# Expert-output row scatters declared independent of each other in a chunk-select attention and top-1 routing kernel

## The chip, the cores and the metric

The kernel runs on one core of one Trainium2 chip. The metric is device time in microseconds (us), the median of several runs. The engines are named as in the profile: PE is the matrix engine, PEld its weight load, DVE the vector engine, ACT the scalar engine, POOL the GpSimd engine and SP the sync engine; POOL and SP issue the transfers that matter here, and 16 DMA engines carry them.

## What is computed

An attention over 4 x 8 heads of 768 positions keeps six chunks of 32 keys per query; its output, reshaped to 3072 tokens of 512 numbers, goes through a mixture of eight experts of which each token uses one.

```python
def _moe_ref(x, w_gate, w1, w2):          # x: 3072 x 512
    logits = x @ w_gate
    expert_idx = np.argmax(logits, axis=1)
    ...
    for e in range(E):                    # 8 experts
        mask = expert_idx == e
        h = np.maximum(x[mask] @ w1[e], 0.0)      # 512 -> 1024
        ye = h @ w2[e]                            # 1024 -> 512
        out[mask] = gate_w[mask, None] * ye
```

## The kernel before

The first part (to about 262 us of the span) is the attention. As token rows are finished they are scattered by expert into a scratch table in HBM, `xs_dram`, with 258 four-byte words a row: the token's 512 bf16 numbers, its gate weight and its number. Some steps of the second part are begun before the first ends.

The second part works through 31 tiles of up to 128 tokens, `j` = 0 to 30, each of one expert. For each tile there are five steps:

- `gather(j)`: an indirect transfer, issued by POOL, brings 128 rows of `xs_dram` into one of eight buffers (four named `xg`, two halves of `KTE`, two of `QSB`). Rows beyond the expert's count have an index out of bounds and are skipped.
- `x_in(j)`: a transposing transfer, issued by SP, turns the tile into `xT` (128 x 512 bf16, kept in the other `KTE` and `QSB`), and DVE copies the token numbers to `ti` (L541 to L547); where a row is no token's the number is made out of bounds.
- `up(j)`: 8 matmuls of 512 columns into `ph` (L558), ACT's Relu into `h` (L562), and a transposing transfer on SP from `h` to `hT` (128 x 1024 bf16, L564).
- `down(j)`: 8 matmuls into `py` (L571), for which there is one buffer; ACT scales `py` into `y` (L575; four buffers in turn).
- still in `down(j)`: an indirect transfer, issued by POOL, scatters the 128 rows of `y` (2 KB each) to `out` in HBM (L576). Rows out of bounds are skipped. Padding makes the last tiles hold few tokens or none.

The order on PE and on SP is the program's; on the other engines the scheduler sets it. The steady order is `gather(j+4)`, `up(j)`, `x_in(j+3)`, `down(j-2)`:

```python
for j in range(NA + 2, JT + 2):
    order += [(up, j), (x_in, j + 3), (down, j - 2)]
for f, j in order:
    if j >= JT:
        continue
    if f is up and j + 4 < JT:
        gather(j + 4)
    f(j)
```

Every engine works through its own list in order, so an instruction that waits holds up all behind it on that engine. The waits are set by a dependency tracker. Two writes to one tensor are ordered by it: it does not know which rows an indirect transfer writes, so each scatter into `out` waits until the scatter before it has landed. A transfer also takes one of eight semaphores in turn (DMASW0 to DMASW7 for POOL's), and waits for the transfer that used it eight transfers earlier.

Of the kernel before, what the change touches and what calls it, by code (L numbers as in the profile page):

```python
# [21 lines left out]
def kernel(  # L22
# [10 lines left out]
    nc = tc.nc  # L33
# [533 lines left out]
    def down(j):  # L567
        hT, wo = fs[j]["hT"], fs[j]["wo"]
        py = ps_o.tile([128, DM], FP32, tag="o")
        for c in range(NFC):  # L570
            nc.tensor.matmul(py[:], lhsT=hT[:, c, :], rhs=w_all[:, ds(wo + (W1W + c * DM), DM)],  # L571
                             start=(c == 0), stop=(c == NFC - 1))
        nm = ("k", "q", "v", "v")[j % 4]
        y = ld.tile([128, DM], FP32, tag=nm, bufs=2 if nm == "v" else 1, name="y")
        nc.scalar.activation(y[:], py[:], AF.Copy, bias=0.0, scale=fs[j]["gt"])  # L575
        nc.gpsimd.indirect_dma_start(  # L576
            out=out[:], out_offset=bass.IndirectOffsetOnAxis(ap=fs[j]["ti"], axis=0),
            in_=y[:], in_offset=None, bounds_check=NTOK - 1, oob_is_err=False,
        )

# [14 lines left out]
    with tc.manual_schedule(engines={PE}):  # L597
# [60 lines left out]
        with tc.manual_schedule(engines={SP}):  # L658
# [10 lines left out]
            up(2)  # L669
            x_in(5)  # L670
            down(0)
            r[1]()
            gather(6)
# [4 lines left out]
            for j in range(3, NA):  # L678
                order += [(up, j)] + [(x_in, j + 3)] * (j + 3 < NA) + [(down, j - 2)]
            order += [(down, NA - 2), (x_in, NA), (x_in, NA + 1), (x_in, NA + 2), (up, NA),  # L680
                      (x_in, NA + 3), (down, NA - 1), (up, NA + 1), (x_in, NA + 4)]
            for j in range(NA + 2, JT + 2):
# [44 lines left out]
```

## Time and profile before

| | us |
|---|---|
| median of 3 runs | 414.83 (412.9 to 415.79) |
| profiled execution | 411.02 |
| its span, first to last instruction | 409.3 |
| PE busy in the span | 351.9 |
| ACT busy | 242.0 |
| DVE busy | 230.0 |
| POOL busy | 187.6 |

The mean granted clock of PE is 0.959 of full speed. The busy shares are means over two parts with different limits; DVE is nearly idle in the second one. What the second part waits for is read from the order of its instructions in time and from the row at the end of the idle stretches, which names what came last.

### The profile page before, as it was taken

What the parts mean: (1) busy time and instruction counts of PE and PEld (TensorE: products, weight loads), DVE (VectorE), ACT (ScalarE), POOL (GpSimd) and SP (SyncE); (2) the same over time, 40 slices, a digit from 0 to 9 for tenths busy, and PEclk for the clock granted to TensorE, in tenths of its full rate; (3) what the DMA queues carried; (4) which work ended last, traced back from release to release, by engine and by line L of the source; (5) the groups of instructions that cost most, each with busy time, mean ns of one, the idle gap of its engine ahead of it and who ended that gap; (6) DMA issues with size and microseconds to landing.
All of it is one profiled execution on the core that took longest, in us unless ns stands there. A gap on an engine that the chain in (4) does not pass through costs nothing.

```text
span 409.3 us, 7510 instructions
## 1 busy us (share of the span) xinstructions
PE 351.9 (86%) x2272; PEld 175.0 (43%) x2272; DVE 230.0 (56%) x783; ACT 242.0 (59%) x403; POOL 187.6 (46%) x304
## 2 busy tenths in 40 slices
PE   2688999999989999799999798899799879988710
PEld 1244455545545545445545444444244334333300
DVE  8449789889978989968989985670000000000000
ACT  2487779779769777849777845244244434443300
POOL 9124244333674424753433746646454353534131
PEclk9889999999999999989999989999899999999975
DMA  9265999898799899699799452479879878877610
GB/s 178 56 117 113 172 184 146 151 204 163 156 197 165 182 169 176 144 197 180 142 172 189 91 105 53 117 136 195 182 183 163 180 133 202 162 174 147 141 43 0
DMA packets 143366, 60.99 MB, mean 149 GB/s; under 512 B 127963, under 2 KB 136157, under 8 KB 143328
## 3 DMA queue, kind: packets, MB, share of 16 engines
q1 hardware_dynamic: 125408, 31.09, 40.6%
q0 software_dynamic: 17920, 29.42, 37.0%
q8 instruction: 20, 0.33, 0.3%
q14 instruction: 18, 0.15, 0.2%
HBM read 56.54 MB, written 11.30 MB: 166 GB/s over the span
## 4 chain that ended last, share of the span: by engine, by line
PE 45%; DMA 21%; ACT 12%; issue 9%; DVE 8%; POOL 2%; POOLq 1%; SPq 0%; ACTq 0%; DVEq 0%
DMA out_dram<-y,ti 16%; PE po L310 11%; PE ps L288 6%; PE ph L558 5%; PE pu L233 5%; PE py L571 3%; ACT Pr L293 3%; PE pu L338 3%; PE pt L370 3%; ACT QSB L262 3%; ACT QSB L261 3%; PE pu L343 2%; PE pt L209 2%; PE pt L241 2%; DMA xg<-xs_dram,grow 2%
## 5 line engine op out<-in xcount | busy, mean ns | idle before, releaser
L322 DVE TENSOR_TENSOR Pa<-Pa,Pr 128x768 f32<-128x768 f32 (+2 forms) x112 | 82.2, 734 | 4.4 <-PE po L310 2.4
L293 ACT ACTIVATE Pr<-ps 128x768 f32<-128x768 f32 (+2 forms) x112 | 65.3, 628 | 3.4 <-PE ps L288 3.1
L297 POOL TENSOR_SCALAR_AFFINE_SELECT Pr<-Pr 128x256 f32<-128x256 f32 x80 | 33.6, 438 | 72.8 <-ACT Pr L293 71.9
L571 PE MATMUL py<-w_all,hT 128*128 x248 | 58.6, 379 | 4.2 <-ACT y L575 2.6
L576 POOL DMA_INDIRECT out_dram<-y,ti x31 | 30.8, 994 | 63.1 <-DMA out_dram<-y,ti 23.2
L288 PE MATMUL ps<-QSB,KTE 128*128 128x384 bf16 (+2 forms) x288 | 49.2, 295 | 3.5 <-ACT QSB L262 2.5
L288 PEld LDWEIGHTS <-KTE 128*128 128x128 bf16 x288 | 24.3, 98 | 35.8 <-issue 27.7
L571 PEld LDWEIGHTS <-hT 128*128 128x128 bf16 x248 | 24.2, 98 | 35.0 <-issue 3.2
L558 PE MATMUL ph<-w_all,KTE 128*128 x128 | 31.9, 394 | 6.2 <-DMA KTE<-xg 3.7
L435 POOL DMA_INDIRECT xs_dram<-xrow,sli x24 | 26.7, 1111 | 13.8 <-DVE sli L428 5.2
L558 PE MATMUL ph<-w_all,QSB 128*128 x120 | 28.1, 379 | 3.8 <-PE py L571 2.9
L546 DVE TENSOR_TENSOR ti<-xg,inv_i 128x1 int32<-128x1 int32 x12 | 1.9, 160 | 51.4 <-DMA xg<-xs_dram,grow 51.4
L346 ACT ACTIVATE ud<-pu 128x384 f32<-128x384 f32 x16 | 7.8, 491 | 34.2 <-PE pu L343 34.2
L293 ACT ACTIVATE Pa<-ps 128x768 f32<-128x768 f32 x32 | 25.9, 811 | 3.2 <-PE ps L288 2.6
L172 POOL DMA_DIRECT2D w_all<-in_moe_w_dram x32 | 24.5, 764 | 0.0
L558 PEld LDWEIGHTS <-KTE 128*128 128x128 bf16 x128 | 12.7, 100 | 23.8 <-issue 7.1
L201 DVE TENSOR_REDUCE kmx<-pt 128x12 f32<-128x384 f32 x32 | 17.7, 554 | 7.5 <-PE pt L199 7.4
L218 POOL CAST QSB<-qT 64x384 bf16<-64x384 f32 x32 | 16.0, 508 | 11.6 <-DVE qT L216 11.2
L244 DVE TENSOR_TENSOR ubm<-pt,cbias 128x144 f32<-128x144 f32 x32 | 8.6, 302 | 21.6 <-PE pt L241 21.5
L529 POOL DMA_INDIRECT xg<-xs_dram,grow x16 | 16.9, 1056 | 6.9 <-issue 6.6
L558 PEld LDWEIGHTS <-QSB 128*128 128x128 bf16 x120 | 11.6, 97 | 19.4 <-issue 5.0
L372 DVE TENSOR_TENSOR xrow<-pt,rec 128x384 bf16<-128x384 f32 x32 | 17.6, 552 | 1.9 <-DMA xs_dram<-xrow,sli 1.1
(296 smaller groups left out, 668.2 us busy)
## 6 DMA issues: line engine op xcount, KB each, us to landing
w_all<-in_moe_w_dram POOLq DMA_DIRECT2D x32, 512.0 KB, 7.3
out_dram<-y,ti POOLq DMA_INDIRECT x31, 3.3
t__187<-in_k_dram SPq DMA_DIRECT2D x2, 192.0 KB, 3.1
t__190<-in_q_dram SPq DMA_DIRECT2D x2, 192.0 KB
t__193<-in_v_dram SPq DMA_DIRECT2D x2, 192.0 KB, 4.1
t__202<-in_v_dram SPq DMA_DIRECT2D x2, 192.0 KB, 4.6
t__196<-in_k_dram SPq DMA_DIRECT2D x2, 192.0 KB, 3.2
t__199<-in_q_dram SPq DMA_DIRECT2D x2, 192.0 KB, 3.4
```

What stands on the lines that cost most here:

```text
L172: d = nc.gpsimd.dma_start(out=dst, in_=src.rearrange("(c p) f -> p c f", p=128))
L201: nc.vector.tensor_reduce(s["kmx"][:, ts(hf, 12)], pk, AX.X, ALU.max)
L233: nc.tensor.matmul(pu[64 * hf:64 * hf + 64, :], lhsT=w_[:], rhs=s[f"{nm}{hf}"][:], start=(nm == "qT"), stop=(nm == "qA"), skip_group_check ...
L288: nc.tensor.matmul(pv[:, hd, :], lhsT=kte[:, hd, ts(kb, 128)], rhs=qsb[:, hd, ds(qb * 384 + 384 - w, w)], start=True, stop=True, skip_grou ...
L293: nc.scalar.activation(P[:, :, ds(c0, w)], pv, AF.Exp)
L297: nc.gpsimd.affine_select(out=pd, in_=pd, pattern=[[0, 2], [1, 128]], compare_op=ALU.is_ge, fill=0.0, base=0, channel_multiplier=-1)
L310: nc.tensor.matmul(po[64 * hd:64 * hd + 64, 384 - w:384], lhsT=vt[:, kb, hd, :], rhs=P[:, hd, ds(c0, w)], start=first, stop=last and n == ...
L322: nc.vector.tensor_tensor(acc[:, :, 384 - w:384], acc[:, :, 384 - w:384], P[:, :, ds(c0, w)], ALU.add)
L435: d = nc.gpsimd.indirect_dma_start(out=xs_dram[:], out_offset=bass.IndirectOffsetOnAxis(ap=sli[:, u:u + 1], axis=0), in_=bst[b][f"xrow{u % ...
L558: nc.tensor.matmul(ph[:, fh, :], lhsT=xT[:, c, :], rhs=w_all[:, ds(wo + (c * F + fh * 512), 512)], start=(c == 0), stop=(c == NDC - 1), sk ...
L571: nc.tensor.matmul(py[:], lhsT=hT[:, c, :], rhs=w_all[:, ds(wo + (W1W + c * DM), DM)], start=(c == 0), stop=(c == NFC - 1))
L576: nc.gpsimd.indirect_dma_start(out=out[:], out_offset=bass.IndirectOffsetOnAxis(ap=fs[j]["ti"], axis=0), in_=y[:], in_offset=None, bounds_ ...
```

## The change

The scatters of `y` are put into a group `y` whose members are declared free of dependencies on one another, because no token is in two tiles. Nothing else is edited.

```diff
         y = ld.tile([128, DM], FP32, tag=nm, bufs=2 if nm == "v" else 1, name="y")
         nc.scalar.activation(y[:], py[:], AF.Copy, bias=0.0, scale=fs[j]["gt"])
-        nc.gpsimd.indirect_dma_start(
+        d = nc.gpsimd.indirect_dma_start(
             out=out[:], out_offset=bass.IndirectOffsetOnAxis(ap=fs[j]["ti"], axis=0),
             in_=y[:], in_offset=None, bounds_check=NTOK - 1, oob_is_err=False,
         )
+        tc.declare_no_dep(d.ins, group="y", reason="every token is in one tile")
+        tc.add_to_no_dep_group("y", d.ins)
```

PE, DVE, ACT and SP keep their instructions in the same order. POOL's list changes in its waits, and in one place in its order. The first place is the middle of the second part, where gathers (L529) and scatters (L576) alternate. Before:

```order
L529 DMA KTE1_169<-xs_dram_63,grow_183 128x258 [waits DMAHW2_49,DMASW3_49]
L529 DMA QSB1_173<-xs_dram_63,grow_183 128x258 [waits DMAHW4_49,Activation_49]
L576 DMA out_0_dram<-y_3968,ti_3808 3072x512 [waits DMASW5_49,DMASW2_49]
L576 DMA out_0_dram<-y_4013,ti_3844 3072x512 [waits DMASW5_49,Activation_49]
L529 DMA QSB1_173<-xs_dram_63,grow_183 128x258 [waits DMAHW6_49,DMASW7_49]
L576 DMA out_0_dram<-y_4071,ti_3974 3072x512 [waits DMASW6_49,DVE_49,Activation_49]
L529 DMA xg0_3507<-xs_dram_63,grow_183 128x258 [waits DMAHW2_49,DMASW1_49]
L576 DMA out_0_dram<-y_4107,ti_3977 3072x512 [waits DMASW0_49,DVE_49,Activation_49]
```

and in the changed kernel, the same stretch of POOL's list:

```order
L529 DMA KTE1_169<-xs_dram_63,grow_183 128x258 [waits DMAHW2_49,DMASW3_49]
L576 DMA out_0_dram<-y_3968,ti_3808 3072x512 [waits DMASW4_49,Activation_49]
L529 DMA QSB1_173<-xs_dram_63,grow_183 128x258 [waits DMAHW4_49,DMASW5_49]
L576 DMA out_0_dram<-y_4013,ti_3844 3072x512 [waits DMASW6_49,Activation_49]
L529 DMA QSB1_173<-xs_dram_63,grow_183 128x258 [waits DMAHW6_49,DMASW7_49]
L576 DMA out_0_dram<-y_4071,ti_3974 3072x512 [waits DMASW0_49,DVE_49,Activation_49]
L529 DMA xg0_3507<-xs_dram_63,grow_183 128x258 [waits DMAHW2_49,DMASW1_49]
L576 DMA out_0_dram<-y_4107,ti_3977 3072x512 [waits DMASW2_49,DVE_49,Activation_49]
```

The scatter of y_3968 (tile 6) moved ahead of the gather of tile 14. The DMA semaphore that each scatter waits for was the one of the scatter before it; it is now the one that it takes itself, last used eight transfers earlier, which is four scatters earlier.

The second place is the end of POOL's list, the last six scatters (tiles 25 to 30). Before:

```order
L576 DMA out_0_dram<-y_4680,ti_4492 3072x512 [waits DMASW7_49,DVE_49,Activation_49]
L576 DMA out_0_dram<-y_4710,ti_4528 3072x512 [waits DMASW0_49,DMASW1_49,DVE_49,Activation_49]
L576 DMA out_0_dram<-y_4740,ti_4564 3072x512 [waits DMASW1_49,DVE_49,Activation_49]
L576 DMA out_0_dram<-y_4770,ti_4600 3072x512 [waits DMASW2_49,DMASW3_49,DVE_49,Activation_49]
L576 DMA out_0_dram<-y_4784,ti_4636 3072x512 [waits DMASW3_49,DVE_49,Activation_49]
L576 DMA out_0_dram<-y_4798,ti_4669 3072x512 [waits DMASW4_49,DMASW5_49,DVE_49,Activation_49]
```

and in the changed kernel:

```order
L576 DMA out_0_dram<-y_4680,ti_4492 3072x512 [waits DMASW0_49,DVE_49,Activation_49]
L576 DMA out_0_dram<-y_4710,ti_4528 3072x512 [waits DMASW1_49,DVE_49,Activation_49]
L576 DMA out_0_dram<-y_4740,ti_4564 3072x512 [waits DMASW2_49,DVE_49,Activation_49]
L576 DMA out_0_dram<-y_4770,ti_4600 3072x512 [waits DMASW3_49,DVE_49,Activation_49]
L576 DMA out_0_dram<-y_4784,ti_4636 3072x512 [waits DMASW4_49,DVE_49,Activation_49]
L576 DMA out_0_dram<-y_4798,ti_4669 3072x512 [waits DMASW5_49,DVE_49,Activation_49]
```

Nothing moved here; each scatter lost the wait for the one before it and keeps those for its own `y` (ACT), its own `ti` (DVE) and the transfer eight earlier.

## Rows read from the trace of the kernel before

**Rows 1.** The page's part 4, chain that ended last: shares by line.

```profile
DMA out_dram<-y,ti 16%; PE po L310 11%; PE ps L288 6%; PE ph L558 5%; PE pu L233 5%; PE py L571 3%; ACT Pr L293 3%; PE pu L338 3%; PE pt L370 3%; ACT QSB L262 3%; ACT QSB L261 3%; PE pu L343 2%; PE pt L209 2%; PE pt L241 2%; DMA xg<-xs_dram,grow 2%
```

**Rows 2.** POOL's timeline, 279 to 409 us: start, duration, instruction, idle before.

```profile
292.41 1.01 POOL L576 DMA_INDIRECT out_dram<-y,ti  x1 [3.10 <-issue]
...
308.95 0.99 POOL L576 DMA_INDIRECT out_dram<-y,ti  x1 [3.75 <-ACT y L575]
310.24 1.05 POOL L529 DMA_INDIRECT QSB<-xs_dram,grow  x1 [0.30 <-issue]
313.84 1.01 POOL L576 DMA_INDIRECT out_dram<-y,ti  x1 [2.54 <-DMA out_dram<-y,ti]
...
398.88 0.97 POOL L576 DMA_INDIRECT out_dram<-y,ti  x1 [1.88 <-DMA out_dram<-y,ti]
401.82 0.97 POOL L576 DMA_INDIRECT out_dram<-y,ti  x1 [1.97 <-DMA out_dram<-y,ti]
```

**Rows 3.** ACT's timeline in the second part.

```profile
299.50 0.69 ACT L575 ACTIVATE y<-py,QSB 128x512 f32<-128x512 f32 x1 [0.75 <-PE py L571]
...
383.79 1.02 ACT L562 ACTIVATE h__4757<-ph 128x1024 bf16<-128x1024 f32 x1 [2.17 <-PE ph L558]
385.52 0.69 ACT L575 ACTIVATE y<-py,KTE 128x512 f32<-128x512 f32 x1 [0.70 <-PE py L571]
...
391.95 0.69 ACT L575 ACTIVATE y<-py,QSB 128x512 f32<-128x512 f32 x1 [2.91 <-DMA out_dram<-y,ti]
```

**Rows 4.** PE's timeline, 289 to 392 us.

```profile
294.14 3.55 PE L558 MATMUL ph<-w_all,KTE 128*128 x8 [2.12 <-DMA KTE<-xg]
...
304.43 1.89 PE L558 MATMUL ph<-w_all,QSB 128*128 x8
...
314.87 1.89 PE L558 MATMUL ph<-w_all,KTE 128*128 x8
...
319.71 1.89 PE L558 MATMUL ph<-w_all,QSB 128*128 x8 [0.45 <-PE py L571]
...
381.82 1.89 PE L558 MATMUL ph<-w_all,KTE 128*128 x8 [0.97 <-PE py L571]
383.54 1.89 PE L571 MATMUL py<-w_all,hT 128*128 x8
...
389.09 1.89 PE L571 MATMUL py<-w_all,hT 128*128 x8 [0.94 <-ACT y L575]
```

**Rows 5.** SP's timeline: the transposing transfer of one `x_in`.

```profile
316.34 1.19 SPq L541 DMA_TRANSPOSE QSB<-QSB  x1
```

**Rows 6.** Windows: us, busy time of each engine, granted clock, DMA share, GB/s.

```profile
300.00:304.00 4.00, 4.00 (x20) 1.75 (x18) 0.16 (x1) 2.23 (x3) 3.06 (x3) 1.00 0.83 200
304.00:308.00 4.00, 4.00 (x20) 1.79 (x19) 0.16 (x1) 1.71 (x2) 1.02 (x1) 1.00 1.07 230
308.00:312.00 4.00, 4.00 (x20) 1.83 (x19) 0.16 (x1) 2.09 (x3) 2.05 (x2) 1.00 0.94 196
300.00:320.00 20.00, 18.94 (x88) 8.37 (x86) 0.79 (x5) 9.73 (x12) 9.37 (x10) 1.00 0.98 185
320.00:340.00 20.00, 17.18 (x78) 7.41 (x77) 0.80 (x5) 7.90 (x10) 9.13 (x10) 1.00 0.80 166
340.00:360.00 20.00, 17.96 (x81) 7.78 (x80) 0.64 (x4) 8.55 (x10) 10.12 (x10) 1.00 0.90 184
360.00:380.00 20.00, 18.02 (x81) 7.67 (x79) 0.80 (x5) 8.55 (x10) 9.18 (x9) 1.00 0.72 154
```

**Rows 7.** Issue to landing: scatters of `y`; transposes into `hT`; gathers (284 to 390 us).

```profile
DMA to landing us min/median/max: 2.1/3.3/4.7
...
DMA to landing us min/median/max: 3.1/3.5/4.5
...
DMA to landing us min/median/max: 2.6/3.5/6.1
```

**Rows 8.** The page's part 3: POOL's queue, with packets, MB, share of 16 engines.

```profile
q0 software_dynamic: 17920, 29.42, 37.0%
```

## The prediction

> **What bounds the kernel now.** Start with the chain of work that ended last. Its largest single share, 16%, is the landing of scatters into `out`, before any engine's line [rows 1]. Busy times alone would not have told this: in the second part PE is busy for 17 to 19 of every 20 us [rows 6]. Next, POOL's timeline shows how the scatters come to be there. The scatter at 308.95 us is that of tile 7, whose `y` ACT wrote from 299.50 us on [rows 2, 3]: it starts 8.8 us after its data were ready, because the scatter before it had first to land. (The row names ACT as what came last; ACT had long been done, so it was another.) The next one starts at 313.84, named as waiting for the landing of its predecessor [rows 2]. So scatters form a chain of their own, of issue (1.0 us) and landing (3.3 us in the middle case [rows 7]), and POOL's list makes others share it: the gather of tile 15 stands right behind the scatter of tile 7 and starts at 310.24 [rows 2]; its `x_in` can start only at 316.34 [rows 5]; its `up` starts at 319.71, 4.84 us after the one before [rows 4].
>
> That is to be set against PE's own pace. A block of eight matmuls takes 1.72 us when the next follows directly (381.82 to 383.54), so an `up` and a `down` take 3.44 us [rows 4]. From `up(11)` at 304.43 to `up(14)` at 314.87 three steps took 10.44 us, 3.48 each; from `up(11)` to `up(30)` at 381.82 nineteen took 77.39 us, 4.07 each [rows 4]. PE thus loses 0.63 us a step, all of it after `up(14)`.
>
> At the end there is nothing but the chain. `down(30)` starts at 389.09 and needs 1.89 us, to 390.98 [rows 4], yet the last scatter starts at 401.82, its predecessor at 398.88 [rows 2].
>
> **The change, part by part.** No instruction is added or removed. What goes is one wait per scatter; what remains is each one's own `y`, its own `ti`, and the transfer eight earlier, which in the steady order is the scatter of four tiles earlier. Four steps are at least 13.8 us, and the longest landing shown is 4.7 us [rows 7], so I cost that wait at nothing; if landings rose above 12 us it would be felt.
>
> *The end.* `y` followed its matmuls by 0.09 us where it waited for nothing else: `down(28)` starts at 383.54, so it ends at 385.43, and `y` starts at 385.52 and takes 0.69 [rows 3, 4]. For tile 30: 390.98 + 0.09 + 0.69 = 391.76, after which its scatter may start, against 401.82: **10.05 us** saved. Before, `y` of tile 30 itself waited, to 391.95, for a scatter to free its buffer [rows 3]; that goes too. The `down`s of the end are 2.7 us or more apart and a scatter keeps POOL 0.97 us, so POOL is no queue there. What comes after the last scatter moves with it unchanged. This term rests on PE's end staying where it is; the next term moves it.
>
> *The nineteen steps.* Gathers no longer stand behind a waiting scatter. They come some 8 us earlier relative to `up`, `x_in` and with it the next `hT` (behind it in SP's list) come on time, and PE's own pace is next: 19 x 3.44 = 65.4 us, 12.0 saved. That is one end. The other is the DMA engines. A step with all its rows moves 132 KB of gather, 131 KB of `x_in`, 262 KB of `hT` and 262 KB of scatter, 787 KB. The busiest twelve microseconds, 300 to 312, with DMA shares of 0.83, 1.07 and 0.94, moved 200, 230 and 196 GB/s, 209 in the mean [rows 6]: 3.77 us for such a step, 71.6 for nineteen, 5.8 saved. Not all steps are full: the four windows from 300 to 380 us moved 185, 166, 184 and 154 GB/s [rows 6], 13.8 MB in 80 us or 19.7 steps of 4.07, that is 700 KB, and 3.35 us at 209 GB/s. So on average the DMA engines can just keep PE's pace, and while full tiles pass they can't quite. Between 3.44 and 3.77 I take **3.6 us** a step: 3.48 was really run for three steps under this load, but with gathers fetched ahead, so that pace was partly paid from a lead. 19 x 3.6 = 68.4, **9.0 us** saved.
>
> The Trainium skill ("DMA: Bandwidth & Descriptors", sections "Bandwidth" and "Latency and other measured facts") gives about 358 GB/s for HBM transfers of a core and 261 GB/s for a transposing transfer; an estimate from these is 393 KB / 261 + 394 KB / 358 = 2.6 us for a full step, well under 3.44, and by it the whole 12.0 us would come back, a time near 393. The best 4 us window here, 230 GB/s over all queues [rows 6], does not bear that out; I stay with the windows.
>
> *The steps ahead of it.* The scatter at 292.41 (tile 3) idled 3.10 us first [rows 2]; it will be issued up to that much earlier, when the `x_in` is under way for which PE waits 2.12 us before `up(8)` at 294.14 [rows 4]. Its 262 KB at 230 GB/s are 1.1 us, the most that it can delay that transfer; the least is nothing. A gain there I exclude, since that `x_in` waits for no scatter into `out`. I take 0.3 us, nearer to nothing, since the scatter's bytes would mostly have passed by then. The exchange of tile 6's scatter with tile 14's gather costs one issue of 1.0 us on POOL, hidden, because the gather is needed two steps later.
>
> **Sum:** 9.0 + 10.05 - 0.3 = 18.75 us. Against the profiled execution's own 411.02 that is 392.3; that execution was 3.8 us below the median of the runs, so for the median I take the difference: 414.83 - 18.75 = **396.1 us**. With the bounds: at best 12.0 + 10.05, 392.8; at worst 5.8 + 10.05 - 1.1 = 14.75, 400.1.
>
> **The rivals.** *The DMA engines become the bound.* Without the chain, scatter, gather and two transposing transfers of a step meet more often, and all of them stretch. For it: shares of 0.9 and more already, and at 1.07 the rate rose only to 230 GB/s [rows 6]. Against: the average step needs 3.35 us. At 3.77 to 4.0 us a step it gives 5.8 to 1.4 us in place of 9.0, so 399.3 to 403.7. The Trainium skill (the same page, "Issuing engines are not separate DMA queues") says that transfers from any engine run on the same 16 DMA engines, which is this rival's premise; the share above 1 beside a nearly level rate agrees.
>
> *Slower: the gathers land late behind free scatters.* Both go through POOL's one queue [rows 8], so a gather issued 1.3 us after a scatter lies behind its bytes. There is a loop: scatter of `j-3`, gather `j+4`, `x_in(j+4)`, `hT` of `j+2` behind it on SP, `down(j+2)`, `y`, scatter of `j+2`: five steps. Its length is 0.99 + 0.30, a gather's landing 3.5 (6.1 at most), 1.19 on SP, `hT` 3.5 (4.5 at most), 1.89, 0.09 and 0.69 [rows 2 to 5, 7]: 12.2 us, at most 15.8, against 17.2 for five steps of PE. To make the kernel slower by 1% it would have to eat the end's 10.05 us and 4.15 more, 0.75 us a step, so 4.82 a step and 24.1 a loop: gathers would have to land 15 us after issue. Time then 419 or more. Nothing in the rows comes near.
>
> *The change does nothing, or its gain is handed on.* The waits for eight transfers earlier could act as the old one did, or steps grow so that PE ends later by what the end saves: 411 to 419. For the first, a landing of over 12 us would be needed; for the second, 4.6 us a step.
>
> **How the numbers follow.** A measurement of this kernel can tell about 1%, 4.1 us, from no change. Forecast (3.44 to 3.68 us a step): 62%. DMA bound (3.68 to 4.0): 32%. Nothing or handed on: 4%. Slower: 2%. So faster 0.94, same 0.04, slower 0.02. The range goes from 391.5 (PE's pace, with 1.3 us for the spread of the runs) to 402, which takes in most of the DMA rival and leaves its last part and the two others outside.
>
> **What would show it.** In the changed kernel's profile, scatters should start within 0.1 us of their `y` or directly behind a gather, and no row should name the landing of `out` as what POOL waits for. The distance from `up(11)` to `up(30)` over 19 should be about 3.6; 3.44 proves PE the bound, 3.77 and more the DMA engines, with `hT` landing in over 4.5 us and DMA shares near 1. The last scatter should start 0.8 us after the last matmul. I am wrong in the first term if another wait holds the last scatters, in the second if transposes land so late that PE idles before `down`, or if `x_in` waits for gathers still.

## The result, and the profile after

The changed kernel took 391.93 us (median of 4 runs, 391.16 to 393.09), the kernel before, run beside it, 415.31 (4 runs, 412.9 to 418.19): a ratio of 0.944, 95% interval 0.937 to 0.950. The forecast was 396.1. The profiled execution took 393.09, its span is 391.4, against 411.02 and 409.3 before. In three later sets of runs the kernel before came to 412.0 to 412.8, and the changed kernel, in two of them, to 398.11 (ratio 0.967, 0.962 to 0.971) and 398.53 (0.968, 0.963 to 0.973). A ratio is that of the means of fast runs, those not over 1.5% above the fastest of their kernel, while a median is of all runs. So the gain is real, and its size moved between occasions; both facts are taken up below.

The page of the changed kernel: the shares by engine and line of the chain that ended last (part 4), and the scatters' row in part 5 (busy time and mean ns, then idle time before them and who ended it). It answers to [rows 1].

```profile
POOL out_dram L576 4%; POOL xg L529 2%; DMA KTE<-xs_dram,grow 2%; POOL QSB L529 1%; POOL KTE L529 1%; DMA QSB<-xs_dram,grow 1%; DMA xg<-xs_dram,grow 1%; DMA out_dram<-y,ti 1%; POOL xs_dram L435 0%; POOLq L724 0%; POOLq L576 0%; DVE ti L546 0%; POOLq L529 0%; DVEq L546 0%
...
L576 POOL DMA_INDIRECT out_dram<-y,ti x31 | 31.2, 1006 | 44.6 <-ACT y L575 42.8
```

The landing of scatters fell from 16% of that chain to 1%. Scatters now wait 42.8 us in all for their own `y`, which is harmless: it is the time until there is something to scatter. No scatter of `y` names the landing of `out` any more.

POOL's timeline of the changed kernel, as [rows 2]:

```profile
289.89 1.02 POOL L576 DMA_INDIRECT out_dram<-y,ti  x1 [0.31 <-issue]
...
308.65 1.02 POOL L576 DMA_INDIRECT out_dram<-y,ti  x1 [2.82 <-ACT y L575]
309.97 1.04 POOL L529 DMA_INDIRECT xg<-xs_dram,grow  x1 [0.30 <-issue]
...
381.18 0.97 POOL L576 DMA_INDIRECT out_dram<-y,ti  x1 [1.74 <-ACT y L575]
383.89 0.97 POOL L576 DMA_INDIRECT out_dram<-y,ti  x1 [1.74 <-ACT y L575]
```

The first row is the scatter of tile 3, 2.5 us earlier than before (292.41). The scatter of tile 8 starts at 308.65; it was 313.84 before. The gather behind it follows after 0.30 us, and the last scatter starts at 383.89 in place of 401.82.

PE's timeline, as [rows 4], with `up(8)`, `up(11)`, `up(14)`, `up(30)` and `down(30)`:

```profile
296.46 3.57 PE L558 MATMUL ph<-w_all,KTE 128*128 x8 [5.07 <-DMA KTE<-xg]
...
307.43 1.89 PE L558 MATMUL ph<-w_all,QSB 128*128 x8
...
318.55 1.89 PE L558 MATMUL ph<-w_all,KTE 128*128 x8 [0.60 <-PE py L571]
...
373.80 1.89 PE L558 MATMUL ph<-w_all,KTE 128*128 x8
...
380.95 1.89 PE L571 MATMUL py<-w_all,hT 128*128 x8 [0.82 <-ACT y L575]
```

From `up(11)` to `up(30)` it is 66.37 us, 3.49 a step against 4.07 before: 11.0 us saved. `down(30)` ends at 382.84, and the last scatter starts 1.05 us later, 10.84 before: 9.8 saved. But `up(11)` itself came 3.0 us later than before (307.43 against 304.43): `up(8)` waited 5.07 us for its `xT`, against 2.12. The sum, 11.0 + 9.8 - 3.0 = 17.8, is the difference of the spans (17.9).

The windows of the changed kernel, as [rows 6], show what bounds it now:

```profile
300.00:320.00 20.00, 19.40 (x88) 8.53 (x86) 0.64 (x4) 9.58 (x11) 9.49 (x10) 0.97 0.87 183
320.00:340.00 20.00, 20.00 (x95) 9.08 (x93) 1.02 (x6) 10.06 (x12) 11.31 (x11) 1.00 0.91 208
340.00:360.00 20.00, 20.00 (x95) 9.02 (x94) 0.96 (x6) 9.78 (x12) 12.22 (x12) 1.00 0.88 192
```

PE is busy for 20.00 of 20 us at a granted clock of 1.00; it was 17.18 and 17.96. From 320 to 340 us the DMA engines move 208 GB/s, as much as in the busiest twelve microseconds before (209), while PE loses nothing.

### The profile page after: what moved, and what is told of

Read it like the earlier page. It is cut to its first block, busy times and chain, and to the rows that moved or that the text cites. A ratio compares the mean times of both kernels' runs of the same rounds, so it can differ in the third digit from the quotient of the medians.

```text
span 391.4 us, 7508 instructions
## 1 busy us (share of the span) xinstructions
PE 349.7 (89%) x2272; PEld 175.3 (45%) x2272; DVE 229.7 (59%) x783; ACT 242.1 (62%) x403; POOL 187.9 (48%) x304
## 5 line engine op out<-in xcount | busy, mean ns | idle before, releaser
L576 POOL DMA_INDIRECT out_dram<-y,ti x31 | 31.2, 1006 | 44.6 <-ACT y L575 42.8
L529 POOL DMA_INDIRECT xg<-xs_dram,grow x16 | 16.8, 1053 | 7.0 <-issue 6.0
L370 PE MATMUL pt<-ident_f,ot 128*128 128x128 f32 x96 | 17.1, 288 | 1.4 <-ACT KTE L204 0.3
```

Of the source, the lines that this page charges most:

```text
L529: d = nc.gpsimd.indirect_dma_start(out=xg_bufs[j % XB].bitcast(I32), out_offset=None, in_=xs_dram[:], in_offset=bass.IndirectOffsetOnAxis( ...
L576: d = nc.gpsimd.indirect_dma_start(out=out[:], out_offset=bass.IndirectOffsetOnAxis(ap=fs[j]["ti"], axis=0), in_=y[:], in_offset=None, bou ...
```

## The experiments

Unless a number says otherwise, all are compared with the kernel before, run beside them. In the first set those had a median of 411.96 us (11 runs), in the second 412.83 (7), in the third 412.31 (17). Spans are those of the profiled execution.

**Which scatters matter.** Three kernels declare only some of the scatters independent; all scatters stay members of the group.

```diff
-        tc.declare_no_dep(d.ins, group="y", reason="every token is in one tile")
+        if j >= 6:
+            tc.declare_no_dep(d.ins, group="y", reason="every token is in one tile")
```

with `j >= 6` (the first six stay in the chain), `j >= 25` (only the last six are free) and `j < 25` (only the last six are chained).

> Only the scatters of tiles 6 to 30 are free; those of tiles 1 to 5 still wait each for the one before. Theory (the freed early scatters crowd the transposing transfers of tiles 8 to 10, so that PE stood for 5.07 us before up(8) in the changed kernel against 2.12 before): up(8) starts near 294 again and the kernel takes about 389 us, 3 less than the changed kernel. Rival (a chance stall of the DMA engines fell there, whoever issues what): up(8) is as late as in the changed kernel, or varies, and the time is 392.

> Only the scatters of tiles 25 to 30 are free. Theory (two separate gains, 10 us at the end and the rest in the steps): the steps keep their 4.07 us, the last scatter starts about 1 us after PE's last matmul, 405 us. Rival (the gain at the end needs free scatters all along): 410 us or more.

> The scatters of tiles 0 to 24 are free, those of tiles 25 to 30 wait each for the one before. Theory (the 10 us at the end were a lag of two tiles gathered over all steps; a chain of six that starts without lag keeps up with tiles that come 3.45 or 2.7 us apart): 393 to 395 us. Rival (the end is serial landings by themselves): six landings in a row again cost about 10 us, 402.

Measured: free from 6 on 397.48 us (6 runs; ratio 0.962, 0.956 to 0.968), the last six free 401.60 (4 runs; 0.977, 0.969 to 0.984), the last six chained 403.95 (4 runs; 0.981, 0.974 to 0.987).

The expected times had counted from 391.93. All profiles of this set have a pause of PE near 280 us, some 7 us long, which those of the first two kernels don't have and which is taken up below. So the times alone decide little here: 397.48 fits neither expectation, and 403.95 is near the rival's 402. What is compared is the distances from `up(11)` on.

With the last six free, POOL's timeline, the scatters of tiles 24 to 30:

```profile
380.07 0.97 POOL L576 DMA_INDIRECT out_dram<-y,ti  x1 [3.12 <-DMA out_dram<-y,ti]
381.34 0.97 POOL L576 DMA_INDIRECT out_dram<-y,ti  x1 [0.30 <-issue]
...
385.17 0.97 POOL L576 DMA_INDIRECT out_dram<-y,ti  x1 [0.30 <-issue]
387.54 0.97 POOL L576 DMA_INDIRECT out_dram<-y,ti  x1 [1.39 <-ACT y L575]
390.25 0.97 POOL L576 DMA_INDIRECT out_dram<-y,ti  x1 [1.74 <-ACT y L575]
```

The first of these rows, tile 24, is the last that waits for a landing. It starts 11.7 us after PE had finished that tile's `down` (366.50 + 1.89 = 368.39). The next four are free and leave behind one another, 1.28 us apart; from tile 29 on each waits for its own `y` alone, and the last starts 1.05 us after PE's end (387.31 + 1.89 = 389.20). So what stands at the end is a queue of finished tiles, and freeing a few scatters works it off in 5.1 us. The theory's 4.07 us a step was wrong: it was 3.63 (`up(11)` at 311.20, `up(30)` at 380.16), for a reason that the kernel before shows below. With the same pause this profile's span, 397.7, is that of the whole change, 398.1; by the medians the last six free are 3.5 us slower (401.60 against 398.11).

With the last six chained, the end of POOL's timeline:

```profile
376.92 0.97 POOL L576 DMA_INDIRECT out_dram<-y,ti  x1 [3.83 <-DMA out_dram<-y,ti]
382.35 0.97 POOL L576 DMA_INDIRECT out_dram<-y,ti  x1 [4.46 <-ACT y L575]
385.80 0.97 POOL L576 DMA_INDIRECT out_dram<-y,ti  x1 [2.48 <-DMA out_dram<-y,ti]
388.66 0.97 POOL L576 DMA_INDIRECT out_dram<-y,ti  x1 [1.89 <-DMA out_dram<-y,ti]
391.60 0.97 POOL L576 DMA_INDIRECT out_dram<-y,ti  x1 [1.97 <-DMA out_dram<-y,ti]
```

PE ends at 384.65 + 1.89 = 386.54 there, so the last scatter starts 5.06 us later: 4.0 more than free, not the rival's 10 more. The same kernel in the second set:

> Scatters of tiles 0 to 24 free, the last six chained, on the same chip as the changed kernel. Theory (corrected by the first run of this kernel, whose last scatter began 5.1 us after PE's last matmul against 1.05): 3 to 5 us over the changed kernel. Rival (six landings in a row cost what they cost before): 10 us over it.

It took 402.08 us (4 runs; 0.978, 0.972 to 0.983). Its last matmuls and its last scatter:

```profile
389.35 1.89 PE L571 MATMUL py<-w_all,hT 128*128 x8 [0.82 <-ACT y L575]
392.98 0.97 POOL L576 DMA_INDIRECT out_dram<-y,ti  x1 [1.97 <-DMA out_dram<-y,ti]
```

The scatter came only 1.74 us after PE's end (391.24). Six landings in a row therefore cost between 0.7 and 4.0 us at the end. The other 6 to 9 us of the kernel before were brought along from the steps. The median lies 4.0 us above that of the whole change in the same set, more than 0.7; its `up(11)` also came 1.6 us later in the profile, so the 4.0 aren't all the chain's.

**Two chains in place of one.** Scatters of even and of odd tiles each keep their own chain:

```diff
-        tc.declare_no_dep(d.ins, group="y", reason="every token is in one tile")
-        tc.add_to_no_dep_group("y", d.ins)
+        tc.declare_no_dep(d.ins, group=f"y{(j + 1) % 2}", reason="every token is in one tile")
+        tc.add_to_no_dep_group(f"y{j % 2}", d.ins)
```

> Each scatter waits for the one two tiles earlier. Theory (a chain binds only where issue and landing, 4 to 4.5 us, exceed the step; two chains have 6.9 us for that): same as the changed kernel, 392 us. Rival (any wait of a scatter for a landing holds up the gathers behind it): a third or more of the gain is lost, 400 us or more.

Measured: 401.17 us (4 runs; 0.974, 0.968 to 0.981). `up(11)`, `up(30)`, `down(30)` and the last scatter:

```profile
315.62 1.89 PE L558 MATMUL ph<-w_all,QSB 128*128 x8
381.23 1.89 PE L558 MATMUL ph<-w_all,KTE 128*128 x8
388.38 1.89 PE L571 MATMUL py<-w_all,hT 128*128 x8 [0.83 <-ACT y L575]
391.32 0.97 POOL L576 DMA_INDIRECT out_dram<-y,ti  x1 [1.74 <-ACT y L575]
```

The steps ran at (381.23 - 315.62) / 19 = 3.45 us, and the last scatter started 1.05 us after PE's end (388.38 + 1.89). From `up(11)` on this is the whole change. The time is the rival's, 400 or more, but not for the rival's reason: no scatter of `y` names a landing. What was lost against 391.93 lies ahead of `up(11)`, which came at 315.62. Part of it is the pause. Against the whole change with the pause (398.11) 3.1 us are left; in the profiles the very first scatter, ahead of any chain, already started 2.3 us later (274.15 against 271.81). So the chain hurts because one issue and one landing, 1.0 + 3.3 us [rows 2, 7], are longer than a step of 3.45; with 6.9 us for each scatter it is no bound.

**The same two kernels again, and where the later sets lost.** The whole change and the kernel before, unedited:

> The changed kernel again, beside the next ones on one chip. In the four runs before, PE stood 6.8 to 7.3 us for ACT near 280 us of the span, in all four and in neither profile of the two kernels. Theory (that stall belongs to the chip or the execution and not to the edits): it can be here too, and then the time is near 399; without it, 392, and then the next kernel shows it no more either.

> The kernel before, with a profile on the same chip. Theory (a stall of PE lets the chain of scatters catch up, so that it costs less here): with the stall near 280 us the time is still 411 to 416, and the step from up(11) to up(30) is shorter than 4.07 us. Rival: the stall adds itself, 418 or more.

Measured: the whole change 398.11 us (4 runs), the kernel before 411.11 in its one profiled run. PE's timeline of the kernel before in that set:

```profile
286.84 3.57 PE L571 MATMUL py<-w_all,hT 128*128 x8 [6.14 <-ACT y L575]
...
302.50 1.89 PE L558 MATMUL ph<-w_all,KTE 128*128 x8 [2.07 <-DMA KTE<-xg]
...
311.41 1.89 PE L558 MATMUL ph<-w_all,QSB 128*128 x7
...
381.78 1.89 PE L558 MATMUL ph<-w_all,KTE 128*128 x7 [0.32 <-PE py L571]
...
389.18 1.89 PE L571 MATMUL py<-w_all,hT 128*128 x8 [1.08 <-ACT y L575]
```

and its POOL timeline, the scatters of tiles 2, 8 and 30:

```profile
287.06 1.02 POOL L576 DMA_INDIRECT out_dram<-y,ti  x1 [2.32 <-ACT y L575]
...
314.31 1.00 POOL L576 DMA_INDIRECT out_dram<-y,ti  x1 [2.87 <-DMA out_dram<-y,ti]
...
401.91 0.97 POOL L576 DMA_INDIRECT out_dram<-y,ti  x1 [1.97 <-DMA out_dram<-y,ti]
```

Here PE stood for 6.14 us ahead of a `down`, a pause that no row of the first two profiles shows: ACT wrote a `y` late. All twelve later profiles have such a pause (5.5 to 7.4 us), whatever the edit; the two first have none. `up(11)` came 7.0 us later than in [rows 4], and yet the span is 409.4 against 409.3. The reason is in POOL's rows. The scatter of tile 8 starts at 314.31 (313.84 in [rows 2]), the last at 401.91 (401.82): 22 intervals of 3.98 us (4.00). The chain of scatters was the clock of the kernel before; PE could be early or late by 7 us, and the chain did not notice. The steps then took 70.37 / 19 = 3.70 us, since PE had less lead to lose.

The changed kernel has no such clock, so the pause shows. Its PE timeline in that set:

```profile
287.21 3.53 PE L571 MATMUL py<-w_all,hT 128*128 x8 [7.43 <-ACT y L575]
...
303.98 3.36 PE L558 MATMUL ph<-w_all,KTE 128*128 x8 [3.61 <-DMA KTE<-xg]
...
314.29 1.89 PE L558 MATMUL ph<-w_all,QSB 128*128 x7
...
380.55 1.89 PE L558 MATMUL ph<-w_all,KTE 128*128 x7
...
387.70 1.89 PE L571 MATMUL py<-w_all,hT 128*128 x8 [0.82 <-ACT y L575]
```

Steps 66.26 / 19 = 3.49; last scatter 390.64, 1.05 us after PE's end. Against the kernel before in that set: steps 4.1 saved, end 9.8, `up(11)` 2.9 later, together 11.0 of a difference of 11.3. The profiled executions of the changed kernel thus lie 6.7 us apart (398.1 against 391.4). That is the larger part of why the ratio is 0.967 here and 0.944 in the first runs; the rest is that the kernel before had a median of 415.31 then and of 412.83 here.

**The DMA engines, with a third more to carry.** The changed kernel, and each `y` from tile 8 on is also stored a second time, to a scratch buffer in HBM, by a transfer that ACT issues:

```diff
+        if j >= 8:
+            nc.scalar.dma_start(out=copy_dram[ds(j * 128, 128), :], in_=y[:])
```

> The changed kernel, with each y from tile 8 on stored a second time, 262 KB in plain rows to a scratch table, issued by ACT. Theory (the DMA engines are nearly full at PE's pace; a step moves 0.96 MB on average, which at 209 to 230 GB/s takes 4.2 to 4.6 us): steps of 4.2 us or more, 14 us or more over the changed kernel. Rival (by the rates of 261 and 358 GB/s a full step with the store takes 3.35 us and PE stays the bound): steps of 3.45 to 3.5 us, at most 2 us over it.

Measured in one run: 408.57 us, span 406.9, 8.8 above the whole change in the same set. Its windows:

```profile
320.00:340.00 20.00, 17.99 (x79) 7.78 (x80) 0.80 (x5) 8.55 (x10) 10.42 (x11) 1.00 1.12 241
340.00:360.00 20.00, 17.17 (x78) 7.59 (x78) 0.80 (x5) 8.56 (x10) 9.55 (x10) 1.00 1.12 248
360.00:380.00 20.00, 18.02 (x82) 7.98 (x83) 0.80 (x5) 8.56 (x10) 9.58 (x10) 1.00 1.13 234
```

`up(11)` and `up(30)`, one line further down in this kernel, of each of which the trace has seven matmuls:

```profile
314.76 1.89 PE L559 MATMUL ph<-w_all,QSB 128*128 x7
389.43 1.89 PE L559 MATMUL ph<-w_all,KTE 128*128 x7 [0.40 <-PE py L572]
```

The steps took (389.43 - 314.76) / 19 = 3.93 us, between what the two theories asked. With 262 KB more the transfers most likely bind, at 241 GB/s and a share of 1.12. (PE's rows name the landing of `hT` for 2.9 us of waiting in these steps; for another 3.0 they name nothing. It is one run.) If they do, the mixture of transfers of this kernel is carried at some 240 GB/s when the DMA engines are the bound; 700 KB then take 2.9 us, and 787 KB, a step with all its rows, 3.3. Both are under PE's 3.45.

The Trainium skill ("DMA: Bandwidth & Descriptors", sections "Bandwidth" and "Latency and other measured facts") gives 358 GB/s as a core's limit for HBM transfers and 261 GB/s for a transposing transfer whose middle dimension is not contiguous. An estimate by these for a full step with the second store, 393 KB transposed and 656 KB to or from HBM, is 393 / 261 + 656 / 358 = 3.3 us, so that it would have cost nothing. The 3.93 us and 241 GB/s measured don't bear that out.

**The steps ahead of `up(11)`.** The first set suggested that free early scatters delay `up(8)`: with the first six chained it had waited 1.88 us and the total was lowest. The test, on one chip: the first six chained, the whole change, the first nine chained, and, last, only the first six free.

```diff
-        tc.declare_no_dep(d.ins, group="y", reason="every token is in one tile")
+        if j < 6:
+            tc.declare_no_dep(d.ins, group="y", reason="every token is in one tile")
```

The others have `j >= 6` and `j >= 9` in that place.

> Scatters 0 to 5 in the chain, 6 to 30 declared independent, beside the whole change on the same chip. Theory (the five scatters issued ahead of their time put their bytes before the loads of tiles 8 to 10): the wait of PE before up(8) is about 2 us and not 3.6, and from the release of the ACT stall to up(11) it takes 23.5 to 24.5 us, against 26 to 27.1 in the whole change; the steps run at 3.45 to 3.5 in both; the span is 2 to 3 us below that of the whole change (ratio of the two medians 0.993 to 0.995). Rival (the lead is spent again on a stall within the steps, or up(8) is late for another reason): medians within 1 us.

> The whole change again, as the comparison for the same call. Theory: 3.49 us a step, last scatter 1.05 us after the last matmul, up(8) waiting 3 to 5 us; 398 us with the stall of ACT near 280 us, 392 without it.

> Scatters 0 to 8 in the chain, 9 to 30 declared independent. Theory: up(8) as in the kernel with 0 to 5 chained, since no scatter from 6 on is issued before up(8) has started; a chain that goes on longer only carries its backlog further, so some steps after up(11) are late by up to 2 us in all: the same as with 0 to 5 chained or up to 2 us slower. Rival (bytes of scatters 6 to 8 matter for the next loads too): 1 us or more faster than with 0 to 5 chained.

> Scatters 0 to 5 declared independent, 6 to 30 in the chain: the early part of the change alone. Theory (the chain holds a backlog at the end and swallows what PE loses earlier): up(8) and up(11) come 2 to 3 us later than in the kernel before relative to the ACT stall, and yet the total is within 1.5 us of the kernel before, because the last scatter follows the chain. Rival (what is lost early is lost at the end): 2 to 3 us slower than before, a ratio of 1.005 to 1.008. A second rival (the first scatters being out earlier shortens the chain): 2 us or more faster.

Measured, medians of 6, 6, 6 and 12 runs: first six chained 398.55 us (ratio 0.966, 0.961 to 0.971), whole change 398.53 (0.968, 0.963 to 0.973), first nine chained 398.11 (0.966, 0.960 to 0.972), only the first six free 414.27 (1.004, 1.001 to 1.008).

The theory falls: it asked for 2 to 3 us, and the medians with the first six chained and with all free differ by 0.02; the intervals leave room for some 2 us either way. The profiles don't bear it out either. PE's timeline of the whole change in this set, the end of the pause, `up(8)` and `up(11)`:

```profile
285.38 3.41 PE L571 MATMUL py<-w_all,hT 128*128 x8 [7.29 <-ACT y L575]
...
300.27 1.89 PE L558 MATMUL ph<-w_all,KTE 128*128 x8 [1.87 <-DMA KTE<-xg]
...
308.90 1.89 PE L558 MATMUL ph<-w_all,QSB 128*128 x8
```

and with the first six chained:

```profile
287.46 3.46 PE L571 MATMUL py<-w_all,hT 128*128 x8 [7.29 <-ACT y L575]
...
303.32 2.62 PE L558 MATMUL ph<-w_all,KTE 128*128 x8 [2.78 <-DMA KTE<-xg]
...
313.63 1.89 PE L558 MATMUL ph<-w_all,QSB 128*128 x8
```

From the end of the pause to `up(11)` it is 23.5 us with free scatters and 26.2 with chained ones, the reverse of the expectation. In the first set the chained kernel had needed 23.6, in the second the whole change 27.1. The whole change's own `up(8)` waited 1.87 us here, where 3 to 5 was expected. So `up(8)` is late in some executions and not in others, in either kernel. The section on the hardware has what goes with it.

With only the first six free, the chain took the delay as in the kernel before: `up(11)` came 26.8 us after the pause (24.6 in the kernel before of the second set), and the scatter of tile 8 still started at 314.03 and the last one 10.85 us after PE's end. The total is nevertheless 2.0 us above the kernel before, more than the 1.5 of the theory and at the lower edge of its rival's 2 to 3. In the one profile the chain was slower behind tile 8 (91.56 us for 22 intervals, 4.16 each); one interval alone, to the scatter of tile 23, took 6.31 us, against 4.69 and 4.04 in the two profiles of the kernel before. Why is not settled.

## Why the prediction was right

The mechanism was right: scatters chained through their landings, gathers behind them in POOL's list, PE waiting for what the gathers feed, and a tail of scatters behind PE's end. The signs named for it are in the profile after, the rivals' are not, with one size off: a scatter starts 0.27 us after the end of its `y` (383.62 to 383.89), not within 0.1. By the terms:

- *The end*, 10.05 us: measured 9.8 (the last scatter from 10.84 to 1.05 us after the last matmul, where 0.8 was forecast). The size is right, less the 0.27 us. What the prediction did not see is that it is a backlog. Chained landings by themselves cost 0.7 to 4.0 us there; the rest is the steps' delay, kept until the end. The end and the steps are thus one thing seen twice, a chain of 4.0 us a link against a step of 3.45.
- *The nineteen steps*, 9.0 us: measured 11.0, 3.49 a step in place of 3.6. The mis-sized number is the DMA engines' 209 GB/s, read from the busiest twelve microseconds and taken as what they can carry. It was what PE's pace asked of them at that moment. The changed kernel moved 208 GB/s with PE fully busy, and with more to carry they reached 241. The step stayed at PE's 3.44, but for one stall of 0.60 us and some tenths.
- *The steps ahead*, a loss of 0.3, at most 1.1: the first profile shows 3.0. The bytes of the scatters, on which the bound rested, are not shown to be the cause: from the pause to `up(11)` the whole change took 23.5 us once and 27.1 once, kernels with the first scatters chained 23.6 to 26.2, and three kernels with early scatters free or chained came within 0.5 us of each other. The bound failed because it knew only one cause; what made `up(8)` late in the first profile is not shown.
- *The sum.* 18.75 us against the spans' 17.9. That it came so near is partly luck: the steps gave 2.0 us more than forecast, the steps ahead took 2.7 more, and the two misses nearly cancelled.
- *The median.* By the profiled executions 392.3 was the sum and 393.09 the measurement. For the median 3.8 us were added, the distance of the kernel before's profile from its median. That spread did not carry over: the changed kernel's 4 runs lay within 391.16 to 393.09. The 396.1 was therefore too high by 4.2, and the range, 391.5 to 402, held the 391.93 by 0.4 us; it held the 398.11 and 398.53 of the later sets as well, but with a pause in them that the prediction knew nothing of.
- *The rivals.* DMA-bound steps were not seen until a third more was moved. Late gathers were not: gathers landed in 3.1 to 4.3 us (6.1 at most before). The gain was not handed on.

## What to carry to other kernels

Where writes to one tensor wait for each other's landing, compare issue plus landing (here 4.0 us a link) with the pace of the loop (3.45): if the link is longer, the chain is the clock, whatever the engines do, and the difference piles up as a tail. Two chains are then as good as none. Freeing a part helps only where it works off the queue: with the last six scatters free the ratio was 0.977, with only the first six free 1.004, where the whole change had 0.967. Such a chain also hides pauses elsewhere, so a gain from cutting it varies with those pauses; and a transfer rate read from a stretch in which another engine sets the pace is a demand and not a capacity.

## What the runs showed of the hardware

**Instruction packets beside a standstill of transfers.** Within 299 to 303 us of the whole change's second profile, in 40 slices of 0.1 us, the mean share of the DMA engines in tenths and the rate, each packet counted in the slice in which it starts, and the queue that carries instructions (packets, MB, share):

```profile
DMA  9929999999999999000000000000006299191999
GB/s 146 100 31 236 289 292 287 250 261 259 253 220 131 197 379 82 0 0 0 0 0 0 5 8 8 10 10 8 10 10 223 82 574 615 41 655 29 284 297 289
...
q8 instruction: 1, 0.02, 1.5%
```

From 300.6 to 302.0 us the engines began next to nothing, though PE was waiting for the `x_in` issued at 298.39. One 16 KB instruction packet starts at 300.3. In both first profiles such packets come every 17 to 25 us in the second part, and packets of other queues took up to 2.3 us at those moments (before: 313.8, 335.6 and 356.7 us; after: 292.2, 315.6, 335.3 and 352.4). The fourteen profiles together have 572 packets of the transposing and of POOL's queue that started from 284 to 390 us and took over 1.3 us; 570 of them overlap such an instruction packet, and the other two lie within 0.04 us of one. Of the 70 instruction packets in that time 40 have such slow packets beside them, and 30 have none. In the fourteen profiles, the packet near the transpose for `up(8)`:

| early scatters | transpose issued | packet starts | idle before `up(8)` | its 8 matmuls |
|---|---|---|---|---|
| chained (before, first) | 290.86 | 289.2 | 2.12 | 3.55 |
| chained (before, second) | 299.23 | 297.6 | 2.07 | 1.89 |
| chained (free from 6) | 299.17 | 297.0 | 1.88 | 1.89 |
| chained (last six free) | 299.06 | 296.9 | 2.03 | 1.89 |
| free (whole change, third) | 296.58 | 294.7 | 1.87 | 1.89 |
| free (last six chained) | 296.58 | 294.3 | 2.90 | 2.82 |
| two chains | 300.96 | 298.7 | 2.92 | 2.85 |
| free (whole change, `y` stored twice) | 302.45 | 300.4 | 1.96 | 1.89 |
| chained (free from 9) | 298.34 | 298.1 | 2.89 | 2.88 |
| chained (free from 6, again) | 298.56 | 299.9 | 2.78 | 2.62 |
| free (last six chained, again) | 300.89 | 302.2 | 2.68 | 2.56 |
| free (whole change, second) | 298.39 | 300.3 | 3.61 | 3.36 |
| free (only the first six) | 296.98 | 298.9 | 3.54 | 3.55 |
| free (whole change, first) | 289.46 | 292.3 | 5.07 | 3.57 |

In all six where the packet starts between 0.3 us before the transpose and 2.9 us after it, PE waits 2.68 us or more. In six of the eight where it was 1.6 to 2.3 us earlier, 2.12 or less; in the two others, 2.9. That is a coincidence of times, and no run moved the packet alone. Whose instructions they are the trace does not say.

**The clock after the wait.** Where `up(8)` takes longer, the granted clock is lower: 0.56 of full speed in the window from 304 to 306 us of the second profile of the whole change, after PE had stood for 3.61 us, so nearer to 1.2 than to 2.4 GHz, and 3.36 us for the eight matmuls; the third profile, after 1.87 us, shows 1.00 and 1.89 us for the same matmuls.

**The pause of ACT near 280 us** (4.6 to 8.4 us idle before the `h` of one tile and 2.0 to 5.4 before the next `y`, in twelve profiles of fourteen) has no cause that the trace shows; the landings of transfers are recorded with gaps there. In all twelve the two stretches add up to 9.8 to 10.3 us, however they are divided, and the twelve come from three different chips. It stays open, and with it why the changed kernel's median was 392 once and 398 twice.
